# Attention and MLP on one core: sums in four column tiles, weights rounded in pieces of 768 columns

## The chip, the cores and the metric

The kernel runs on one core of a Trainium2 chip. The metric is the device time of one launch in microseconds. Five engines work beside each other: PE (matrix products), DVE and POOL (elementwise work[...]), ACT (activations, copies) and SP (issues the DMAs).

## What is computed

```python
# q, k, v: (8, 12, 448, 64); w_in: (768, 2048), w_out: (2048, 768); weights arrive as float64
q_n, k_n = rmsnorm(q, g_q), rmsnorm(k, g_k)
scores = q_n @ k_n.T / 8
attn = exp(scores - max) ; attn = attn / (sum(attn) + 1e-9)
x = (attn @ v), heads side by side          # (8 * 448, 768)
h = x @ w_in
out = (h - tanh(h)) @ w_out                 # (3584, 768)
```

## The kernel before

All values are held transposed: rows on the free axis, d (or the feature) on the partitions. There are 48 steps `s`, one for each pair of heads of each of the 8 batches, six pairs to a batch. A step's attention is cut into `norm` (squares on POOL, their sums on DVE, the power -1/2 on POOL), `norm_q` (q times its factor, DVE), `turn` (k and q transposed by PE, copied by ACT), `scores` (two halves, exponentials on ACT), `add` (sums of the exponentials over four chunks of keys, from step 8 on), `totals` (sums over keys by products with ones), `values` (products with v) and `divide`. The output of `divide` is `xT[b, hp]`, 128 rows (two heads of 64) by 448 queries; for the second three pairs of a batch it also forms the differences `tt` that the fast matrix product needs (on DVE for batch 0, on POOL later).

The MLP is a stream (`mlp`) of single matmuls: `hidden` and `project`, each made of sets of seven products of half size (Strassen-Winograd), 128x128 by 224 columns. A product's result is taken from PSUM by ACT or DVE (`use`). Batch 0's projection (`project_first`) uses plain matmuls of 448 columns instead, 96 of them, counted by `m`.

Everything is in an order written out by hand; each engine runs its own instructions in that order. Slots -3 to 5 (`first_slot`) hold batch 0's attention and no MLP. In slots 6 to 11 (`slot`) the attention of batch 1 is interleaved with batch 0's MLP, in slots 12 to 47 (`late_slot`) that of the following batches with the MLP of the batch before; `run(gap)` takes so much of the stream. The last batch's MLP follows alone.

The weights come as float64 words. A piece is loaded (`weight_load`), then rounded to float32 in three steps: `round_weight_a` on ACT (L71, L72), `round_weight_b` on DVE (L78, L79, L82), `round_weight_c` on POOL (L90). A piece has 384 columns of values; there are 64 of them, 32 of w_in and 32 of w_out. `weight(n)` does step a of piece n-1 and step b of the piece before it; `finish_weights` does step c, for the first `EARLY` = 16 pieces one piece further behind. These 16 are loaded into the place of the tile `gT`, the others into four buffers `w_raw`. In the small slots the number `ahead` says how far to go, later each product of batch 0 asks for its share (`due`). After eight pieces `combine_weights` forms the seven factors of a set; `keep_weights` writes them to DRAM.

The second half of `project_first` forms the factors of w_out: `combine_w_out` (L279, L281, L282 on DVE, L280 on POOL) at every fourth matmul, into slots of a ring of six tiles. Three of the seven factors are blocks of w_out itself; `keep_w_out` writes each of them to DRAM (192 KB) four pieces after it was rounded. The other four are written (`keep_factors`) one combination later. From batch 1 on the products read their factors from DRAM through the ring (`ring_load`), five tiles ahead; the first four loads are issued at m = 86.

In `first_slot` and `slot`, `totals` gives 128 rows by 448: each head's sums repeated over its 64 rows, so that one reciprocal (L427) and one product (L464) finish the step. In `late_slot`, `totals_by_halves` uses four column tiles of 32 and halves of the queries: 128 rows by 224, half the PE time and half the reciprocal (L442). Its rows do not stand where `divide` needs them, so `rows_out` writes four rows to DRAM and `rows_in` reads them back spread over 128 partitions.

Of the kernel before, what the change touches and what calls it, by code (L numbers as in the profile page):

```python
# [20 lines left out]
NCH = 4  # L21
# [71 lines left out]
def bounded_path(tc, ctx, q, k, v, moe_w_in, moe_w_out, out, g_col, ident, ones, neg_half):  # L93
# [14 lines left out]

    nc = tc.nc
# [11 lines left out]
    EARLY = 16  # L121
# [60 lines left out]
    NSTAGE = CF * S // DM  # L182
# [10 lines left out]
    def weight_piece(n):  # L193

        if n < 2 * CF:
            j, f, blk = n // 8, n % 8 // 4, n % 4
            p, low, i = ((1, 0, 0), (0, 1, 0), (4, 1, 1), (2, 0, 1))[blk]
            return 2 * j + f + low * HF, i, built(j, p)[:, f]
        i, f = 1 - (n - 2 * CF) // CF, n % CF
        if i == 0:  # L200
            f = f // 2 + f % 2 * HF
        return f, i, w_out_row(f, i)

    def weight_load(n):

        f, i, _ = weight_piece(n)
        if n < EARLY:
            raw = stage[:, n % NSTAGE * DM : (n % NSTAGE + 1) * DM].rearrange("p (f w) -> p f w", w=2)
        else:
            raw = wp.tile([P, HALF, 2], I32, name="w_raw", bufs=4)  # L210
        if n < 2 * CF:
            rows = w_in_words[i * HALF : (i + 1) * HALF, f * 2 * P : (f + 1) * 2 * P]
            nc.sync.dma_start(
                out=raw.rearrange("p (c f) w -> p c (f w)", c=HC),
                in_=rows.rearrange("(c p) f -> p c f", p=P),
            )
        else:
            nc.sync.dma_start(
                out=raw.rearrange("p f w -> p (f w)"),
                in_=w_out_words[f * P : (f + 1) * P, 2 * i * HALF : 2 * (i + 1) * HALF],  # L220
            )
        raws[n] = raw
# [4 lines left out]
    def place_free(n):  # L227

        if n < EARLY:
            return n - NSTAGE < done[2]  # L230
        return n - 4 < max(done[2], EARLY)

    def weight(to):

        while done[1] < min(to, 4 * CF):
            n = done[1]
            round_weight_a(nc, raws[n], weight_piece(n)[2])
            if n:
                round_weight_b(nc, raws[n - 1], weight_piece(n - 1)[2])
            done[1] = n + 1  # L240
            finish_weights(n - 1 if n < EARLY else n)
            while done[0] < min(n + 6, 4 * CF) and place_free(done[0]):
                weight_load(done[0])
                done[0] += 1
            if kept[1] < kept[0] and n >= 8 * kept[0] + 3:
                keep_weights()
        if done[1] == 4 * CF > done[2]:
            round_weight_b(nc, raws[4 * CF - 1], weight_piece(4 * CF - 1)[2])
            finish_weights(4 * CF)

    def finish_weights(to):
        while done[2] < to:
            round_weight_c(nc, raws.pop(done[2]), weight_piece(done[2])[2])
            done[2] += 1
            if done[2] % 8 == 0 and done[2] <= 2 * CF:
                combine_weights(done[2] // 8 - 1)
            keep_w_out(done[2] - 4)
# [15 lines left out]
    def combine_w_out(f):  # L273

        a11, a21 = (w_out_row(f, i) for i in range(2))
        a12, a22 = (w_out_row(f + HF, i) for i in range(2))
        t = [ring_slot() for _ in range(2)]
        s3, s1, s2, s4 = (t[i // 2][:, i % 2 * HALF : (i % 2 + 1) * HALF] for i in range(4))
        nc.vector.tensor_tensor(out=s1, in0=a21, in1=a22, op=ALU.add)  # L279
        nc.gpsimd.tensor_tensor(out=s3, in0=a11, in1=a21, op=ALU.subtract)  # L280
        nc.vector.tensor_tensor(out=s2, in0=s1, in1=a11, op=ALU.subtract)  # L281
        nc.vector.tensor_tensor(out=s4, in0=a12, in1=s2, op=ALU.subtract)  # L282
        late["keep"].append(lambda: [keep_factors(3 + 2 * i, 2, f, t[i]) for i in range(2)])

    def keep_factors(n, count, f, src):
        nc.sync.dma_start(
            out=w_out_dram[:, n : n + count, :, f, :].rearrange("p k c d -> p (k c) d"),
            in_=src[:, : count * HALF].rearrange("p (k d) -> p k d", d=P),
        )

    def keep_w_out(n):

        if not 2 * CF <= n < 4 * CF:
            return
        f, i, src = weight_piece(n)
        blk = {(0, 0): 0, (HF, 0): 1, (HF, 1): 2}.get((f // HF * HF, i))
        if blk is not None:
            keep_factors(blk, 1, f % HF, src)
# [106 lines left out]
    def values(s, av):  # L405
        v_nat = loaded.pop(("v", s))
        for c in range(NCH):
            p = probs[s, c // 2]
            for h in range(2):
                nc.tensor.matmul(  # L410
                    av[h * D : (h + 1) * D, :S], lhsT=v_nat[:, h, c, :], rhs=p[:, h, c % 2, :],
                    start=(c == 0), stop=(c == NCH - 1),
                )
        return av

    def totals(s, dn):
# [3 lines left out]
        for i, p in enumerate(parts):  # L420
            for h in range(2):
                nc.tensor.matmul(  # L422
                    dn[h * D : (h + 1) * D, :S], lhsT=ones[:CP, :D], rhs=p[:, h, :],
                    start=(i == 0), stop=(i == len(parts) - 1),
                )
        rd = whole[s] = sp.tile([P, S], F32, name="rd")
        nc.vector.reciprocal(rd, dn[:, :S])  # L427

    def totals_by_halves(s, dn):

        t = sums.pop(s)
        parts = t if t else [probs[s, c // 2][:, :, c % 2, :] for c in range(NCH)]
        for i, p in enumerate(parts):
            for h in range(2):
                for n in range(2):
                    r = (2 * h + n) * BL
# [7 lines left out]
    def rows_out(s):  # L444
        rs = whole[s]
        row = whole[s] = scratch.tile([2, S], F32, name="row", bufs=2)
        nc.sync.dma_start(
            out=row.rearrange("h (n q) -> (h n) q", n=2), in_=rs.rearrange("(g i) q -> g i q", i=BL)[:, 0, :]
        )

    def rows_in(s):

        row = whole[s]
        rd = whole[s] = sp.tile([P, S], F32, name="rd")
        nc.sync.dma_start(
            out=rd,
            in_=bass.AP(tensor=row.tensor, offset=row.offset, ap=[[S, 2], [0, D], [1, S]]),
        )

    def divide(s, av):  # L460
        b, hp = steps[s]
        rd = whole.pop(s)
        x = xT[b, hp] = xp.tile([P, S], F32, name="xT")
        nc.vector.tensor_tensor(  # L464
            out=x.rearrange("r (p c) -> r c p", c=NCH), in0=av[:, :S].rearrange("r (c p) -> r c p", c=NCH),
            in1=rd.rearrange("r (c p) -> r c p", c=NCH), op=ALU.mult,
        )
# [17 lines left out]

    due = [min(EARLY + m + 1, 3 * 8) for m in range(9)]
    due += [3 * 8 + m + 1 for m in range(8)]
    due += [2 * CF + CF * (m + 1) // 11 for m in range(11)]
    assert len(due) == 7 * SETS and due[-1] == 3 * CF
# [7 lines left out]
    def products(b, layer, count, width, depth, moving, done_with):  # L497
# [8 lines left out]
        def product(j, p, bank, first):  # L506
            if b == 0:
                weight(due[7 * j + ORDER.index(p)])
                w = built(j, p).rearrange("p f (c d) -> p (f c) d", d=P)
# [3 lines left out]
            for f in range(width):  # L513
                for c in range(depth):
                    nc.tensor.matmul(  # L515
                        bank[:, f * HS : (f + 1) * HS], lhsT=w[:, f * depth + c, :], rhs=moving[p](c),
# [19 lines left out]
    def hidden(b):  # L536
# [17 lines left out]
        def done_with(j):  # L554
            up, down = slice(2 * j, 2 * j + 2), slice(HF + 2 * j, HF + 2 * j + 2)
            s1, s2, s5, u3 = part("s1"), part("s2"), part("s5"), part("u3")
# [14 lines left out]
            def use(p, bank):  # L571
# [9 lines left out]
                elif p == 7:  # L581
                    nc.vector.tensor_tensor(out=u3, in0=v, in1=s5, op=ALU.add)
                    nc.vector.tensor_tensor(out=s1, in0=v, in1=s1, op=ALU.add)

                    def rest():
                        shrink(down, high, u3, nc.gpsimd)
# [31 lines left out]
    def project(b):  # L618
# [7 lines left out]
        def done_with(j):  # L626
            y1, y2, s1, s5 = (part(n).rearrange("p f s -> p (f s)") for n in ("s2", "u3", "s1", "s5"))

            def use(p, bank):
# [3 lines left out]
                elif p == 5:  # L633
                    nc.vector.tensor_tensor(out=s5[:, low], in0=v, in1=s1[:, low], op=ALU.add)
# [4 lines left out]
                elif p == 7:  # L639
                    nc.vector.tensor_tensor(out=y2[:, high], in0=v, in1=s5[:, low], op=ALU.add)  # L640
# [12 lines left out]
    def project_first(b):  # L653
# [6 lines left out]
        for m in range(CD * CF):  # L660
# [4 lines left out]
            if k < HC:  # L665
                weight(3 * CF + CF * (m + 1) // (HC * CF))
            elif m < HC * CF + 4:
                keep_w_out(4 * CF - 4 + m - HC * CF)
            elif (m - HC * CF) % 4 == 0 and m - HC * CF <= 4 * HF:
                for fn in late["keep"]:  # L670
                    fn()
                late["keep"] = []
                combine_w_out((m - HC * CF) // 4 - 1)
            elif m == CD * CF - 12:
                for fn in late["keep"]:
                    fn()
            elif m == CD * CF - 10:
# [13 lines left out]
    def mlp():  # L691
        late["todo"], late["keep"] = [], []
# [30 lines left out]
    def first_slot(s):  # L723
# [8 lines left out]
        ahead = 3 * (s + 4) if s < 0 else 9 + (EARLY - 9) * (s + 1) // NP  # L732
        weight(ahead - 2)
# [4 lines left out]
        weight(ahead - 1)  # L738
# [33 lines left out]
    def late_slot(s):  # L772
        gap = gap_ns(s)
        totals_by_halves(s, sc_bank())
# [5 lines left out]
        rows_out(s)  # L780
# [3 lines left out]
        rows_in(s)  # L784
# [15 lines left out]
    for n in range(4):  # L800
        weight_load(n)
    done[0] = 4
# [235 lines left out]
def kernel(  # L1038
# [45 lines left out]
    ones = consts.tile([P, D], F32, name="ones")  # L1084
# [41 lines left out]
```

## Time and profile before

| | |
|---|---|
| time, median of 3 | 1537.23 us (1536.94 to 1537.45) |
| the profiled execution | 1537.23 us, span 1535.0 us |
| busy PE | 1470.6 us |
| busy DVE | 783.0 us |
| busy POOL | 618.8 us |
| busy ACT | 425.7 us |
| DMA | 255.41 MB, mean 166 GB/s |

A matmul in float32 is recorded twice[...], so 16 records are 8 matmuls. In a timeline row the first number is the start in us from the span's start, the second the length of the merged group, then engine, line, operation, output<-inputs, shapes and how many; in brackets the idle time of the engine before it and what ended it. In a row of groups the numbers after the bar are busy us and mean ns of one, then the idle time before them. L numbers are lines of the kernel before.

### The profile page before, as it was taken

The page shows a single profiled execution, that of the slowest core. Times are in us where ns is not written, and L with a number is a line of the kernel's source. Part 1 is how long each engine was busy: PE and PEld are TensorE (multiplying, and loading weights), DVE is VectorE, ACT ScalarE, POOL GpSimd, SP SyncE. Part 2 cuts the span into 40 slices and gives each one's busy share as a digit, 9 for nine tenths or more (in the row PEclk, how much of TensorE's full clock was granted, in tenths as well). Part 3 has the DMA queues.
Part 4 walks back from the last instruction along what each step waited for, and adds up shares of the span by engine and source line. Part 5 has one row for each costly group of instructions (what it writes and reads, how often), then busy time and mean ns, then how long its engine had stood idle before and what let it go on. Part 6 is the DMA issues. An engine that isn't in the chain of part 4 may idle for free.

```text
span 1535.0 us, 20449 instructions
## 1 busy us (share of the span) xinstructions
PE 1470.6 (96%) x7584; PEld 1156.3 (75%) x7584; DVE 783.0 (51%) x1110; ACT 425.7 (28%) x817; POOL 618.8 (40%) x463
## 2 busy tenths in 40 slices
PE   3999879999999999999999999999999999999998
PEld 1346654448788788878878878887887887889997
DVE  6777888774544365345543455434543354432321
ACT  4463334422322133122221223212232132210100
POOL 5655556634443244432443333432453335311310
PEclk9999989999999999999999999999999999999999
DMA  7534557786456655565455564565556555456563
GB/s 193 160 99 158 179 173 188 190 240 188 159 161 167 172 160 162 154 184 166 147 177 159 165 180 149 159 165 172 161 159 179 151 165 165 138 154 179 181 199 100
DMA packets 255448, 255.41 MB, mean 166 GB/s; under 512 B 143324, under 2 KB 203756, under 8 KB 255340
## 3 DMA queue, kind: packets, MB, share of 16 engines
q1 hardware_dynamic: 255016, 254.01, 56.6%
q8 instruction: 63, 1.03, 0.3%
q14 instruction: 45, 0.37, 0.1%
q10 hardware_dynamic: 324, 0.00, 0.0%
HBM read 220.60 MB, written 33.36 MB: 165 GB/s over the span
## 4 chain that ended last, share of the span: by engine, by line
PE 75%; DVE 14%; DMA 4%; POOL 3%; issue 2%; SPq 2%; ACT 0%; DVEq 0%; ACTq 0%; POOLq 0%
PE mm L515 54%; PE sc L384 8%; PE sc L410 7%; DVE w_out L79 2%; POOL sq L337 1%; DVE rd L427 1%; DVE rr L338 1%; PE sc L437 1%; PE mm L422 1%; POOL rr L342 1%; DVE w_out L82 1%; PE mm L410 1%; DVE w_out L78 1%; PE sc L364 1%; DVE sum L403 1%
## 5 line engine op out<-in xcount | busy, mean ns | idle before, releaser
L389 ACT ACTIVATE p<-sc,rr 112x448 f32<-112x448 f32 x384 | 212.3, 636 | 483.4 <-PE sc L384 407.9
L515 PE MATMUL mm<-xT,w_f 128*128 128x224 f32 x1392 | 280.5, 356 | 4.7 <-DVE s L576 2.7
L515 PEld LDWEIGHTS mm<-xT,w_f 128*128 128x128 f32 x1392 | 261.3, 191 | 23.0 <-issue 14.6
L515 PEld LDWEIGHTS mm<-gT,w_f 128*128 128x128 f32 x1344 | 251.3, 190 | 23.7 <-issue 14.0
L515 PE MATMUL mm<-gT,w_f 128*128 128x224 f32 x1344 | 267.8, 355 | 0.0
L515 PE MATMUL mm<-tt,w_f 128*128 128x224 f32 x1044 | 215.6, 357 | 5.6 <-DVE gT L552 3.2
L515 PEld LDWEIGHTS mm<-tt,w_f 128*128 128x128 f32 x1044 | 197.1, 192 | 16.6 <-issue 8.0
L515 PE MATMUL mm<-tg,w_f 128*128 128x224 f32 x1008 | 200.4, 353 | 0.0
L515 PEld LDWEIGHTS mm<-tg,w_f 128*128 128x128 f32 x1008 | 189.5, 190 | 0.0
L384 PE MATMUL sc<-qT,kT 64*112 64x448 f32 x768 | 178.8, 574 | 9.1 <-DVE rd L427 6.4
L552 POOL TENSOR_TENSOR gT<-s,th 128x448 f32<-128x448 f32 x64 | 77.7, 1214 | 232.1 <-ACT th L551 232.1
L342 POOL TENSOR_TENSOR rr<-rr,neg_half 112x16 f32<-112x16 f32 (+1 forms) x49 | 140.0, 2857 | 51.0 <-DVE rr L341 50.0
L337 POOL TENSOR_TENSOR sq<-q_nat 112x512 f32<-112x512 f32 x48 | 50.0, 1041 | 255.5 <-DVE rr L338 247.3
L384 PEld LDWEIGHTS sc<-qT,kT 64*112 64x112 f32 x768 | 64.0, 176 | 103.8 <-issue 81.9
L410 PE MATMUL sc<-p,v_nat 112*64 112x448 f32 x672 | 135.2, 544 | 0.0
L464 DVE TENSOR_TENSOR xT<-sc,rd 128x448 f32<-128x448 f32 x42 | 40.7, 970 | 127.3 <-PE sc L410 115.1
L338 DVE TENSOR_REDUCE rr<-sq 112x8 f32<-112x512 f32 x96 | 64.9, 676 | 78.3 <-POOL sq L337 78.2
L403 DVE TENSOR_TENSOR sum<-sum,p 112x896 f32<-112x896 f32 x80 | 97.0, 1213 | 12.8 <-ACT p L389 7.9
L478 POOL TENSOR_TENSOR tt<-xT,tt 128x224 f32<-128x224 f32 x21 | 24.7, 1176 | 186.8 <-DVE xT L464 186.8
L410 PEld LDWEIGHTS sc<-p,v_nat 112*64 112x64 f32 x672 | 45.1, 137 | 71.7 <-issue 69.6
L679 PE MATMUL mm<-gT,w_out 128*128 128x448 f32 x192 | 76.1, 549 | 2.1 <-POOL w_out L90 2.1
L551 ACT ACTIVATE th<-s 128x448 f32<-128x448 f32 x64 | 37.1, 579 | 117.8 <-DVE s L595 57.7
(106 smaller groups left out, 1486.9 us busy)
## 6 DMA issues: line engine op xcount, KB each, us to landing
w_f<-w_in SPq DMA_DIRECT2D x196, 384.0 KB
w_f<-w_out SPq DMA_DIRECT2D x147, 512.0 KB
w_raw<-in_moe_w_out_dram SPq DMA_DIRECT2D x32, 384.0 KB
k_nat<-in_k_dram SPq DMA_DIRECT2D x96, 112.0 KB
q_nat<-in_q_dram SPq DMA_DIRECT2D x48, 224.0 KB
v_nat<-in_v_dram SPq DMA_DIRECT2D x48, 224.0 KB
out_dram<-th SPq DMA_DIRECT2D x192, 56.0 KB
w_in<-w_out SPq DMA_DIRECT2D x21, 384.0 KB
```

The lines of the kernel that those rows point to most:

```text
L337: nc.gpsimd.tensor_tensor(out=sq, in0=rows, in1=rows, op=ALU.mult)
L338: nc.vector.reduce_sum(rr[:, "kq".index(name)], sq, axis=AX.X)
L342: nc.gpsimd.tensor_tensor(out=r, in0=r, in1=neg_half[:, : r.shape[1]], op=ALU.pow)
L384: nc.tensor.matmul(sc[:CP, :S], lhsT=kT[r, c * CP : (c + 1) * CP], rhs=qT[r, :], start=True, stop=True)
L389: nc.scalar.activation(p[:, h, i, :], tiles[h][:CP, :S], AF.Exp, scale=rr[:, 0, 2 * c + h : 2 * c + h + 1])
L403: nc.vector.tensor_tensor(out=t, in0=t, in1=part, op=ALU.add)
L410: nc.tensor.matmul(av[h * D : (h + 1) * D, :S], lhsT=v_nat[:, h, c, :], rhs=p[:, h, c % 2, :], start=(c == 0), stop=(c == NCH - 1),)
L464: nc.vector.tensor_tensor(out=x.rearrange("r (p c) -> r c p", c=NCH), in0=av[:, :S].rearrange("r (c p) -> r c p", c=NCH), in1=rd.rearrange ...
L515: nc.tensor.matmul(bank[:, f * HS : (f + 1) * HS], lhsT=w[:, f * depth + c, :], rhs=moving[p](c), start=(first and f == 0 and c == 0), sto ...
L551: nc.scalar.activation(th, h, AF.Tanh, bias=0.0, scale=1.0)
L552: eng.tensor_tensor(out=g[:, rows, cols], in0=h, in1=th, op=ALU.subtract)
L679: nc.tensor.matmul(bank[:, :S], lhsT=w_out_row(f, n // HC)[:, n % HC * P : (n % HC + 1) * P], rhs=g[:, f, :], start=(f == 0), stop=(f == C ...
```

## The change

Four things are changed together.

- `values` uses four column tiles of 32 (two halves of d by two heads) instead of two of 64. Row (m, h, r) of x is then d = 32 m + r of head h; w_in's rows are loaded in that order, in four DMAs of 32 partitions per piece. `totals` of all slots uses four tiles by halves of the queries, rows (n, h). `divide` multiplies in four pieces of 64 rows by 224 queries, where the two inputs can be on different partitions. `rows_out` and `rows_in` are gone.
- A piece of weights has 768 columns: 32 pieces. `EARLY` is 8, `w_raw` has three buffers of twice the size. `finish_weights(n)` no longer lags in the early slots. `ahead` and `due` are set anew.
- `keep_w_out` is gone: `combine_w_out` writes all seven factors of a row, its own blocks among them, in five DMAs right behind it; it stands at every fifth matmul from m = 48. The first ring loads stand at m = 92.
- The tile `u3` is gone, `s5` is used in place.

```diff
-    EARLY = 16
+    EARLY, PIECES = 8, 2 * CF
-    NSTAGE = CF * S // DM
+    NSTAGE = CF * S // (2 * DM)
...
-            raw = wp.tile([P, HALF, 2], I32, name="w_raw", bufs=4)
+            raw = wp.tile([P, 2 * DM], I32, name="w_raw", bufs=3)
...
+            rows = w_in_words[i * HALF : (i + 1) * HALF, f * 2 * P : (f + 2) * 2 * P]
+            rows = rows.rearrange("(c h m r) f -> m h r c f", c=HC, h=2, m=2)
+            for r in range(4):
+                nc.sync.dma_start(
+                    out=raw[r * BL : (r + 1) * BL].rearrange("p (c f) -> p c f", c=HC), in_=rows[r // 2, r % 2]
+                )
...
-            finish_weights(n - 1 if n < EARLY else n)
-            while done[0] < min(n + 6, 4 * CF) and place_free(done[0]):
+            finish_weights(n)
+            while done[0] < min(n + 4, PIECES) and place_free(done[0]):
...
-            keep_w_out(done[2] - 4)
...
-        late["keep"].append(lambda: [keep_factors(3 + 2 * i, 2, f, t[i]) for i in range(2)])
+        for n, count, src in ((0, 1, a11), (1, 1, a12), (2, 1, a22), (3, 2, t[0]), (5, 2, t[1])):
+            nc.sync.dma_start(
+                out=w_out_dram[:, n : n + count, :, f, :].rearrange("p k c d -> p (k c) d"),
+                in_=src[:, : count * HALF].rearrange("p (k d) -> p k d", d=P),
+            )
...
-            for h in range(2):
-                nc.tensor.matmul(
-                    av[h * D : (h + 1) * D, :S], lhsT=v_nat[:, h, c, :], rhs=p[:, h, c % 2, :],
-                    start=(c == 0), stop=(c == NCH - 1),
-                )
+            for m in range(2):
+                for h in range(2):
+                    r = (2 * m + h) * BL
+                    nc.tensor.matmul(
+                        av[r : r + BL, :S], lhsT=v_nat[:, h, c, m * BL : (m + 1) * BL], rhs=p[:, h, c % 2, :],
+                        start=(c == 0), stop=(c == NCH - 1),
+                    )
...
-        nc.vector.tensor_tensor(
-            out=x.rearrange("r (p c) -> r c p", c=NCH), in0=av[:, :S].rearrange("r (c p) -> r c p", c=NCH),
-            in1=rd.rearrange("r (c p) -> r c p", c=NCH), op=ALU.mult,
-        )
+        for n in range(2):
+            for m in range(2):
+                nc.vector.tensor_tensor(
+                    out=x[m * D : (m + 1) * D].rearrange("r (p c) -> r c p", c=NCH)[:, 2 * n : 2 * n + 2],
+                    in0=av[m * D : (m + 1) * D, n * HS : (n + 1) * HS].rearrange("r (c p) -> r c p", c=2),
+                    in1=rs[n * D : (n + 1) * D].rearrange("r (c p) -> r c p", c=2), op=ALU.mult,
+                )
...
-    due = [min(EARLY + m + 1, 3 * 8) for m in range(9)]
-    due += [3 * 8 + m + 1 for m in range(8)]
-    due += [2 * CF + CF * (m + 1) // 11 for m in range(11)]
+    due = [EARLY + m // 2 + 1 for m in range(8)] + [12]
+    due += [12 + m // 2 + 1 for m in range(8)]
+    due += [CF + HF * (m + 1) // 11 for m in range(11)]
...
-            elif (m - HC * CF) % 4 == 0 and m - HC * CF <= 4 * HF:
-                for fn in late["keep"]:
-                    fn()
-                late["keep"] = []
-                combine_w_out((m - HC * CF) // 4 - 1)
...
-            elif m == CD * CF - 10:
+            elif (m - HC * CF) % 5 == 0 and m - HC * CF < 5 * HF:
+                combine_w_out((m - HC * CF) // 5)
+            elif m == CD * CF - 4:
                 ring_load(4)
...
-        ahead = 3 * (s + 4) if s < 0 else 9 + (EARLY - 9) * (s + 1) // NP
-        weight(ahead - 2)
+        ahead = (1, 3, 4, 4, 5, 6, 6, 7, 8)[s + 3]
+        weight(ahead - 1)
...
-        totals_by_halves(s, sc_bank())
+        totals(s, sc_bank())
...
-        rows_out(s)
...
-        rows_in(s)
```

## The prediction

> **What bounds the kernel now.** I read the page first, its slices, then busy time by stretch. The stretches are cut at the divisions (L464) that end a slot: 51.8 us is slot 0's, 107.4 slot 5's, 291.3 slot 10's; at 340.2 the late slots begin.
>
> ```profile
> PE   3999879999999999999999999999999999999998
> ...
> DVE  6777888774544365345543455434543354432321
> ```
>
> ```profile
> 0.00:51.80 51.80, 24.12 (x90) 10.72 (x92) 32.04 (x49) 20.30 (x40) 33.77 (x29) 0.93 0.63 172
> 51.80:107.40 55.60, 53.62 (x282) 20.82 (x284) 43.47 (x60) 31.59 (x63) 29.90 (x20) 1.00 0.48 148
> 107.40:291.30 183.90, 162.64 (x667) 106.02 (x667) 154.67 (x221) 81.00 (x164) 102.27 (x82) 0.94 0.60 177
> 291.30:340.20 48.90, 46.81 (x151) 22.11 (x150) 43.17 (x53) 11.14 (x22) 27.54 (x24) 1.00 0.68 188
> 340.20:1535.00 1194.80, 1183.45 (x6401) 996.58 (x6400) 509.67 (x730) 281.66 (x531) 425.37 (x311) 1.00 0.56 164
> ```
>
> Columns: stretch, length, busy time of PE, PEld, DVE, ACT, POOL, then clock, DMA share, GB/s. After 340 us PE is 99% busy: only PE work itself, or a new stall, counts there. Before it PE idles 46 us, and from 107 to 291 DVE is 84% busy. The timeline of DVE and POOL in slot 4 shows what one small slot hangs on:
>
> ```profile
> 97.93 0.68 DVE L348 TENSOR_TENSOR n<-q_nat,rr 112x512 f32<-112x512 f32 x1
> 98.53 0.35 DVE L78 TENSOR_SCALAR w_out<-w_out 128x384 f32<-128x384 f32 x1
> 98.92 0.36 DVE L79 TENSOR_SCALAR w_out<-w_out 128x384 int32<-128x384 int32 x1
> 99.31 0.56 DVE L82 SCALAR_TENSOR_TENSOR w_out<-gT,w_out 128x384 int32<-128x384 int32 x1
> 99.79 0.68 DVE L338 TENSOR_REDUCE rr<-sq 112x8 f32<-112x512 f32 x1
> 101.62 0.69 DVE L338 TENSOR_REDUCE rr<-sq 112x8 f32<-112x512 f32 x1 [1.15 <-POOL sq L337]
> ...
> 105.75 1.05 DVE L79 TENSOR_SCALAR w_out<-w_out 128x384 int32<-128x384 int32 x1
> ```
>
> ```profile
> 94.86 1.04 POOL L337 TENSOR_TENSOR sq<-k_nat 112x512 f32<-112x512 f32 x1
> ...
> 105.53 1.05 POOL L90 TENSOR_TENSOR w_out<-w_out,gT 128x384 int32<-128x384 int32 x1
> ```
>
> The square of k (94.86) is done long before its sum (99.79), since no rounding stands ahead of it on POOL. And L79 takes 0.36 alone, 1.05 beside L90. In the middle slots the order is another; the chain of waits there:
>
> ```profile
> 157.52 0.70 DVE w_out L78
> 158.22 1.33 issue
> ...
> 160.52 1.05 POOL sq L337
> ...
> 161.60 0.70 DVE rr L338
> 162.36 1.05 POOL sq L337
> ```
>
> The rounding's last addition (L90), then both squares, stand in series with DVE. Durations, by shape:
>
> ```profile
> L427 DVE RECIPROCAL rd<-mm 128x448 f32<-128x448 f32 x6 | 17.7, 2955 | 1.8 <-PE mm L422 1.8
> ...
> L442 DVE RECIPROCAL rs<-sc 128x224 f32<-128x224 f32 x36 | 56.0, 1555 | 10.9 <-PE sc L437 10.9
> ...
> L464 DVE TENSOR_TENSOR xT<-sc,rd 128x448 f32<-128x448 f32 x42 | 40.7, 970 | 127.3 <-PE sc L410 115.1 <-DMA rd<-row 11.6
> ...
> L641 DVE TENSOR_TENSOR s<-mm,s 128x224 f32<-128x224 f32 x21 | 8.0, 381 | 0.0
> ```
>
> And two rows of PE's timeline, four tiles of 32 and two of 64:
>
> ```profile
> 725.85 0.59 PE L437 MATMUL sc<-sum,ones 112*32 112x224 f32 x8
> 710.21 3.23 PE L410 MATMUL sc<-p,v_nat 112*64 112x448 f32 x16
> ```
>
> [...]
>
> **Part by part.** The sum is in the span, 1535.0 us; the profiled execution took 1537.23 with 2.2 us around it, which is also the median.
>
> *Sums over values (48 slots).* 32 records in quads in place of 16 in pairs. A pair starts every 0.375 us (3.16 to the next group), L437's quads start as fast: 0. If not, see the last rival. *Sums over keys.* Slots 0 to 7: 3.16 becomes 8 quads of 224, 1.6, saving 1.58 each; slots 8 to 11: 0.81 to 0.52. PE loses 13.8 us, which counts only where PE sets the slot. Late slots: same matmuls, 0.
>
> *Reciprocal and division.* Twelve reciprocals fall by 1.4. Each division becomes four of 64x224 to a strided output. 0.970 against 0.622 unstrided at 448 puts stride at 0.35, so 0.175 at 224: 0.39 + 0.175 = 0.56, and 0.49 from start to start: 2.04 in place of 0.87, +1.2 on DVE (bounds: 1.5 to 2.4 in all).
>
> *DMA.* 36 rows out and 36 in go, with SP's waits for the reciprocal. The idle column of PE's groups names no DMA there: 0. w_in's loads become 64 issues for 32, at about 0.45 us 13 us more on SP over 230 us; v and k loads stand behind them, but a slot or more ahead of use, which hides it: 0 (all 13 if that lead were gone). The 24 own-block writes of w_out (19 of them before 291) move behind the first half of the projection.
>
> *Double pieces (768 columns).* Alone a piece costs DVE 1.22 us from start to start[...]. POOL's addition has no visible fixed part: 1.05 becomes 2.1. And `finish_weights(n)` puts piece n-1's addition right behind its DVE steps in the early slots too, where it lagged a piece. It blocks POOL's next squares.
>
> Stage by stage:
>
> 1. *To slot 0's division (51.8).* Before, two and three single pieces stand ahead of the first two norms' products (L348: 16.4, 26.9, 38.5 us). Now it is none, one double, none. The second then starts near 24: its sums are scaled by 20.6 (22.2 before, POOL's squares starting 1.2 earlier), the double rounding beside POOL's power takes some 3.2. Two double additions hold POOL to 29.7, so the third norm's sums are scaled at 33.3 (33.8 before) and its product, with no piece between, comes at 36.5 instead of 38.5 and unhindered by additions (L348 took 2.45 there): PE goes on at 37.3, not 41.1. The sums over keys take 2.4 there for 4.8, but the reciprocal waits for DVE's sums to 45.3, and the division comes at about 47.3: -4.5 (bounds -7, +1).
> 2. *Slots 0 to 5 (55.6).* A slot with a double: division 2.04, L348 0.6, rounding 2.1, addition 2.2, squares and sums 3.8, reciprocal 1.5 = 12.3; from slot 3 on tt adds 1.3: 13.7. Without a double PE sets it: 10.0, or 11.2 with tt. Doubles end slots 1, 2, 4; slot 1 also has the combination with its POOL step, +2.4. So 10.0 + 14.7 + 12.3 + 11.2 + 13.7 = 61.9: +6.3 (bounds 0, +10).
> 3. *Slot 5 to 6 (22.8).* Three doubles, where four single pieces were left: 2 more single pieces' work, 2.4, and the longer addition ahead of the norm, 1.0; less 0.2: +3.2.
> 4. *Slots 6 to 10 (161.1).* 42 pieces become 21: -8.4. [...] The addition ahead of the squares, +1.0 in four slots; two combinations beside a longer addition, +1.0. Reciprocal and division together -0.2 in four. DVE's two waits behind late weights (3.7 and 2.5) shrink, -1.5: with three doubles in place of four pieces in flight loads lead little more. Sum -5.7 (bounds -18, +4).
> 5. *To 340.* DMA share 0.68 of 48.9 is 33 us. 19 writes more, 384 packets of 512 bytes at 27 ns over 16 engines, 0.65 us each: +12.3, together 0.93. The combinations (every five matmuls, not four) need ring slots back from such writes; the first ring tile stands behind them. Its load stands at m = 92, not 86, behind k and q: +2.5 (bounds -1, +9).
> 6. *Late slots.* Behind the division wait the sums (L401, L403) and products' results. Two products, 4.5 us, cover them; the queue grows from 4.4 to 5.6 us. Half of the 36 slots divide in the hidden layer with its short products, and one in seven of them by 1 us: +2.5 (bounds -2, +15).
>
> Sum: -4.5 + 6.3 + 3.2 - 5.7 + 2.5 + 2.5 = +4.3. Span 1539.3, time 1541.5: slower by 0.3%. Measurement can't tell 0.2% (3.1 us) from no change.
>
> **Rivals.**
> *DVE's relief wins.* If norms rarely follow a fresh piece, POOL's addition is off the chain: stages 2 and 3 cost 0 and -1, stage 4 about -10.5, the rest -4.5 + 1 + 0: -15, time 1522. For it: DVE is the bound there. Against: the chain above shows L90 ahead of the squares. It decides once stages 2 to 4 together cost 7.3 us less than in my sum.
> *Late stalls.* If each late division costs PE 0.5 us: 18 in place of 2.5, time 1557. Against: the L515 groups waited 16 us in the whole run (4.7, 5.6, 5.9), most of it before 340.
> *Write burst.* If the writes back up 10 us ahead of the ring's first tile: 1549. For: DMA share 0.93. Against: the first ring load was issued at 336.8 and its product began at 342.5, 5.7 us of cover.
> *The tiles don't do it.* If quads ran as two pairs at 448: 48 x 3.0 = +144, 1681. L437 speaks against.
>
> **How the numbers follow.** Likeliest (1541.5, own range 1534 to 1549) 0.45; relief 0.28; late stalls 0.13; burst 0.11; tiles and others 0.03. Range 1521 to 1557: from relief to late stalls. Faster: 0.25 of relief and 0.03 of the likeliest, 0.28. Same: 0.13 of the likeliest and 0.03 of relief, 0.16. Slower: 0.56.
>
> **What would show it.** The first division at about 47 us; the sixth at 109; DVE waiting over 3 us for POOL's squares in slots 2 and 5; the seventh division near 135; late slots at PE 99% with 3.2 us for 32 records. Wrong: POOL's squares still early in the small slots, or L79 waiting less per column than now.

## The result and the profile after

| | before | changed |
|---|---|---|
| time, median of 4 runs | 1537.3 us (1536.94 to 1537.45) | 1551.87 us (1551.0 to 1554.08) |
| ratio, 95% interval | | 1.0097 (1.008 to 1.0115) |
| the profiled execution, span | 1535.0 us | 1552.1 us |

The changed kernel is 14.6 us slower. The profiled execution of it was the slowest of the four (1554.08 us), so the stages below add up to 17.1 us in the span. The two or three us too many can lie in the first stretches, which vary between kernels that are the same there (50.1, 48.3 and 49.0 us to the first division in three of them).

Cut at the same events as in the prediction (the divisions are L434 now, four records each; L numbers in a view are lines of the kernel that it shows), in us:

| stage | before | after | difference | forecast |
|---|---|---|---|---|
| 1. to slot 0's division | 51.8 | 50.1 | -1.7 | -4.5 |
| 2. to slot 5's | 55.6 | 67.9 | +12.3 | +6.3 |
| 3. to slot 6's | 22.8 | 25.9 | +3.1 | +3.2 |
| 4. to slot 10's | 161.1 | 147.4 | -13.7 | -5.7 |
| 5. to the first late slot's sums | 48.9 | 55.1 | +6.2 | +2.5 |
| from there to the first product of batch 1 | 2.3 | 13.6 | +11.3 | in 5 |
| 6. the rest | 1192.5 | 1192.1 | -0.4 | +2.5 |

Two views of the profile after show it: the slices, and the busy time by stretch (columns as before: PE, PEld, DVE, ACT, POOL, then clock, DMA share, GB/s).

```profile
PE   3778889997999999999999999999999999999998
...
DVE  3658888873545456435654455544653555532321
```

```profile
50.10:118.00 67.90, 53.35 (x451) 22.67 (x451) 44.47 (x66) 33.74 (x60) 33.73 (x20) 0.90 0.58 148
118.00:143.90 25.90, 18.89 (x126) 13.34 (x124) 21.13 (x26) 9.76 (x16) 13.60 (x8) 0.89 0.13 31
143.90:291.30 147.40, 132.69 (x647) 89.01 (x648) 123.22 (x141) 63.37 (x97) 86.83 (x51) 0.93 0.62 183
291.30:346.40 55.10, 51.75 (x181) 24.57 (x179) 47.50 (x56) 11.96 (x21) 32.10 (x23) 0.94 0.70 190
346.40:360.00 13.60, 2.33 (x17) 0.80 (x17) 2.89 (x3) 2.74 (x5) 1.44 (x2) 0.74 0.99 258
360.00:1552.00 1192.00, 1181.89 (x6960) 992.84 (x6960) 565.78 (x835) 278.52 (x526) 442.77 (x310) 1.00 0.54 157
```

PE has 14.6 us without work in the small slots (0 to 5), where it had 2.0, and its clock is 0.90 there in place of 1.00. From 346.4 to 360.0 PE does 2.33 us of work while the DMA engines are full. The late slots are as long as before, though their divisions take DVE 1.4 us more each.

**The wait of 11.3 us.** SP's timeline ahead of the late slots, and PE's at their start:

```profile
287.57 0.70 SPq L220 DMA_DIRECT2D w_raw<-in_moe_w_out_dram  x1
304.64 1.90 SPq L584 DMA_DIRECT2D out_dram<-th  x4
306.59 1.57 SPq L290 DMA_DIRECT2D w_out<-w_out  x3
...
345.48 3.84 SPq L584 DMA_DIRECT2D out_dram<-th  x4
349.36 1.58 SPq L290 DMA_DIRECT2D w_out<-w_out  x3
351.05 1.11 SPq L290 DMA_DIRECT2D w_out<-w_f  x2
352.25 2.46 SPq L163 DMA_DIRECT2D k_nat<-in_k_dram  x2
354.76 0.68 SPq L166 DMA_DIRECT2D q_nat<-in_q_dram  x1
355.48 1.88 SPq L318 DMA_DIRECT2D w_f<-w_in  x4
```

```profile
346.97 1.76 PE L379 MATMUL sc<-qT,kT 64*112 64x448 f32 x8
360.02 2.21 PE L486 MATMUL mm<-xT,w_f 128*128 128x224 f32 x5 [11.29 <-DMA w_f<-w_in]
```

SP stood 16.3 us at an output's store (L584 at 304.64, which waits for DVE's transposition th), and no write of w_out could be issued in that time. All 24 own blocks came behind it. The ring's first load was issued at 355.48, and its product followed 4.5 us later. In the kernel before, the same load and its product:

```profile
336.84 3.33 SPq L323 DMA_DIRECT2D w_f<-w_in  x4
...
342.46 2.54 PE L515 MATMUL mm<-xT,w_f 128*128 128x224 f32 x12
```

The busy time by stretch says what SP's wait left idle and what came after it, first in the changed kernel, then in the kernel before:

```profile
287.60:304.60 17.00, 13.65 (x38) 6.32 (x37) 15.43 (x18) 5.97 (x9) 12.03 (x9) 0.92 0.24 67
304.60:320.00 15.40, 15.40 (x45) 7.82 (x45) 14.92 (x19) 3.90 (x7) 9.56 (x6) 0.87 0.71 190
320.00:346.40 26.40, 26.40 (x110) 12.28 (x108) 19.60 (x25) 3.79 (x7) 13.18 (x11) 1.00 1.01 275
```

```profile
287.60:301.00 13.40, 11.31 (x34) 5.02 (x33) 12.99 (x17) 5.51 (x11) 9.27 (x9) 1.00 0.47 156
301.00:320.00 19.00, 19.00 (x68) 8.69 (x67) 17.29 (x23) 3.80 (x7) 11.19 (x8) 1.00 0.86 231
320.00:340.20 20.20, 20.20 (x63) 9.85 (x62) 16.45 (x18) 3.80 (x7) 9.97 (x8) 1.00 0.73 205
```

In the changed kernel the DMA share is 0.24 in the 17 us in which SP waited, then 0.71, then 1.01: the DMA engines first had little to do and then were full until 360. Before, the share was 0.73 when the ring's loads were issued. The store waited because th stands behind the last roundings on DVE, which was busy for 15.43 of those 17.0 us. That this wait made the burst is read from the trace; what an experiment below tests is the place of the writes.

**The small slots.** DVE and PE in slots 3 and 4, from their timelines:

```profile
89.25 2.32 DVE L434 TENSOR_TENSOR xT<-mm,rs 64x224 f32<-64x224 f32 x4
91.61 0.60 DVE L448 TENSOR_TENSOR tt<-xT 128x224 f32<-128x224 f32 x1
...
93.16 0.69 DVE L343 TENSOR_TENSOR n<-q_nat,rr 112x512 f32<-112x512 f32 x1
...
98.19 1.56 DVE L426 RECIPROCAL rs<-mm 128x224 f32<-128x224 f32 x1 [1.70 <-PE mm L421]
104.19 1.17 DVE L434 TENSOR_TENSOR xT<-mm,rs 64x224 f32<-64x224 f32 x2 [4.45 <-PE mm L407]
```

```profile
93.99 0.98 PE L359 MATMUL sc<-ident,n 112*128 112x112 f32 x4 [3.16 <-DVE n L343]
94.90 3.22 PE L421 MATMUL mm<-p,ones 112*32 112x224 f32 x32
98.05 2.93 PE L379 MATMUL sc<-qT,kT 64*112 64x448 f32 x8
...
109.20 1.72 PE L421 MATMUL mm<-p,ones 112*32 112x224 f32 x32
```

In the kernel before, in slot 4:

```profile
98.76 0.57 PE L364 MATMUL sc<-ident,n 112*128 112x112 f32 x4 [0.84 <-DVE n L348]
99.26 3.23 PE L422 MATMUL mm<-p,ones 112*64 112x448 f32 x16
```

No piece is rounded in slot 3, and still it took 14.9 us in this execution (14.8 and 13.4 in the profiles of two runs below, whose code is the same there). Division (2.3) and tt stand ahead of n (L343), and PE waits 3.16 us for n where it had waited 0.84. Then the sums over keys take 3.22 us, as long as in the old form, where the same 32 records take 1.72 one slot later. PE's clock is 0.77 in this slot and 1.00 in the next. That the wait brought the lower clock is a guess from their order; it is not tested, and after a wait of 2.35 us in the next slot the clock did not fall. The reciprocal, shorter by 1.4, ends at 99.8; the division waits till 104.19 for the values. Its gain is beside PE.

**The relief in stage 4.** Groups of one engine by shape, the rounding of w_out, and L79 in the kernel before:

```profile
L90 POOL TENSOR_TENSOR w_out<-w_out,w_raw 128x768 int32<-128x768 int32 x20 | 41.9, 2095 | 46.2 <-DVE w_out L82 21.2 <-issue 9.5 <-ACT w_out L71 5.7
...
L79 DVE TENSOR_SCALAR w_out<-w_out 128x768 int32<-128x768 int32 x28 | 27.1, 969 | 1.0
L82 DVE SCALAR_TENSOR_TENSOR w_out<-w_raw,w_out 128x768 int32<-128x768 int32 x20 | 21.5, 1075 | 0.7
L78 DVE TENSOR_SCALAR w_out<-w_out 128x768 f32<-128x768 f32 x28 | 21.3, 759 | 0.1
```

```profile
L79 DVE TENSOR_SCALAR w_out<-w_out 128x384 int32<-128x384 int32 x56 | 43.3, 773 | 1.9
```

A double piece took DVE 0.76 + 0.97 + 1.08 = 2.8 us. All rows of L78, L79 and L82 together: 118.3 us before for 64 pieces (1.85 each), 87.0 now for 32 (2.72 each). Two effects are in this. Alone, a double piece takes 2.06 us from start to start where two single ones take 2 x 1.22, 0.38 less. And less time went beside POOL: in stage 4, L79 took longer than alone (0.36 us, 0.56 for a double piece) in 21 of 42 pieces before and in 7 of 20 double ones after, each time while an instruction ran on POOL, and what it took above that fell from 15.2 to 7.4 us.

### The profile page after: what moved, and what is told of

Its sections match the earlier page's. It is cut to its first block, busy times and chain, and to the rows that moved or that the text cites. A ratio compares the mean times of both kernels' runs of the same rounds, so it can differ in the third digit from the quotient of the medians.

```text
span 1552.1 us, 22055 instructions
## 1 busy us (share of the span) xinstructions
PE 1463.1 (94%) x8496; PEld 1153.6 (74%) x8496; DVE 823.5 (53%) x1158; ACT 419.0 (27%) x753; POOL 636.5 (41%) x431
## 4 chain that ended last, share of the span: by engine, by line
PE 75%; DVE 10%; POOL 4%; issue 4%; DMA 2%; SPq 1%; ACT 1%; DVEq 0%; POOLq 0%; ACTq 0%
PE mm L486 56%; PE sc L379 8%; PE sc L407 7%; POOL sq L332 2%; DVE rr L333 1%; POOL rr L337 1%; PE sc L421 1%; DVE xT L434 1%; DVE w_out L79 1%; DVE rs L426 1%; PE sc L359 1%; DVE sum L398 1%; POOL gT L523 1%; PE sc L355 1%; DVE w_out L82 1%
## 5 line engine op out<-in xcount | busy, mean ns | idle before, releaser
L486 PE MATMUL mm<-xT,w_f 128*128 128x224 f32 x1392 | 282.2, 357 | 16.5 <-DMA w_f<-w_in 11.3
L523 POOL TENSOR_TENSOR gT<-s,th 128x448 f32<-128x448 f32 x96 | 120.7, 1264 | 262.9 <-ACT th L522 262.9
L486 PEld LDWEIGHTS mm<-tt,w_f 128*128 128x128 f32 x1044 | 195.5, 190 | 12.5 <-issue 8.0
L434 DVE TENSOR_TENSOR xT<-sc,rs 64x224 f32<-64x224 f32 x168 | 94.0, 559 | 128.0 <-PE sc L407 123.7
L407 PE MATMUL sc<-p,v_nat 112*32 112x448 f32 x1344 | 134.8, 542 | 0.0
L449 POOL TENSOR_TENSOR tt<-xT,tt 128x224 f32<-128x224 f32 x21 | 29.0, 1381 | 208.3 <-DVE xT L434 208.3
L398 DVE TENSOR_TENSOR sum<-sum,p 112x896 f32<-112x896 f32 x80 | 107.3, 1342 | 9.1 <-ACT p L384 0.8
L522 ACT ACTIVATE th<-s 128x448 f32<-128x448 f32 x96 | 55.5, 579 | 169.9 <-DVE s L562 62.7
L407 PEld LDWEIGHTS sc<-p,v_nat 112*32 112x32 f32 x1344 | 40.0, 109 | 72.7 <-issue 70.0
```

The costliest lines, as they stand in the source:

```text
L398: nc.vector.tensor_tensor(out=t, in0=t, in1=part, op=ALU.add)
L407: nc.tensor.matmul(av[r : r + BL, :S], lhsT=v_nat[:, h, c, m * BL : (m + 1) * BL], rhs=p[:, h, c % 2, :], start=(c == 0), stop=(c == NCH - 1),
L434: nc.vector.tensor_tensor(out=x[m * D : (m + 1) * D].rearrange("r (p c) -> r c p", c=NCH)[:, 2 * n : 2 * n + 2], in0=av[m * D : (m + 1) * ...
L486: nc.tensor.matmul(bank[:, f * HS : (f + 1) * HS], lhsT=w[:, c * width + f, :], rhs=moving[p](c), start=(first and f == 0 and c == 0), sto ...
L522: nc.scalar.activation(th, h, AF.Tanh, bias=0.0, scale=1.0)
L523: eng.tensor_tensor(out=g[:, rows, cols], in0=h, in1=th, op=ALU.subtract)
```

## The experiments

All times are medians, each beside runs of the kernel before on the same chip (1537.06 to 1537.65 us). "The five slots" is the time from slot 0's division to slot 5's: 55.6 us before, 67.9 in the changed kernel.

**The addition behind its rounding again a piece late.**

```diff
-            finish_weights(n)
+            finish_weights(n - 1 if n < EARLY else n)
```

> The changed kernel, but the last step of the rounding (POOL's addition) of the first eight pieces lags one piece again, so that it no longer stands between a fresh DVE rounding and the squares. Theory A (the addition ahead of k's square is what lengthens the small slots, and PE's lower clock there, 0.74 to 0.77 in two slots, follows from PE's waits): from the first to the sixth division 67.9 us becomes 57 to 61, those slots run at clock 0.95 or more, and the whole falls by 6 to 11 us, to about 1543. Rival B (DVE's own work is what is longer: four divisions of 0.59 us and a double piece in one slot): 67.9 stays above 65 and the whole above 1549.

1548.22 us, five slots 61.9, their clock 0.92. Between the two: 6.0 us of the 12.3 go in the slots as profiled, 3.7 in the medians of the whole (the changed kernel was profiled in its slowest execution, this one in its fastest). The order of POOL's addition is part of the cause, at most half of it; slots 3 and 4 stay at 13.3 us each, and ahead of the first of them PE waits 3.5 us for n.

**Own blocks written as they are rounded.**

```diff
+            keep_w_out(done[2] - 2)
...
-        for n, count, src in ((0, 1, a11), (1, 1, a12), (2, 1, a22), (3, 2, t[0]), (5, 2, t[1])):
+        for i in range(2):
+            keep_factors(3 + 2 * i, 2, f, t[i])
```

> The changed kernel, but w_out's own blocks are written to DRAM two pieces after they are rounded, as before, and a combination writes only its four sums. Theory W (24 writes of 192 KB crowd the 50 us ahead of the first ring loads): PE's wait of 11.3 us for w_f falls under 3 us, the division before the late slots comes no later, and the whole falls by 8 to 13 us, to about 1541. Rival V (the DMA volume only moves, and the loads of w_raw in slots 7 to 10 wait for it instead): the 11.3 us go, but the stretch from the seventh to the eleventh division (147.4 us) grows by 6 us or more, and the whole stays above 1547.

1542.59 us, 9.3 less than the changed kernel. From the start of PE's last projection matmul to the first product of batch 1: 4.7 us (14.0 in the changed kernel, 2.7 before). PE's wait for w_f there is 1.99 us. Stage 4 took 147.7 us, as long as without the writes, though its DMA share rose from 0.62 to 0.69. Theory W holds: the place of the 24 writes costs 9.3 us, and in stage 4 there was room for them. What is left of the wait is the place of the loads, still behind k and q in SP's timeline:

```profile
339.87 1.00 SPq L294 DMA_DIRECT2D w_out<-w_f  x2
340.96 2.14 SPq L163 DMA_DIRECT2D k_nat<-in_k_dram  x2
343.15 0.67 SPq L166 DMA_DIRECT2D q_nat<-in_q_dram  x1
343.87 1.88 SPq L332 DMA_DIRECT2D w_f<-w_in  x4
```

**The first ring loads at m = 86.**

```diff
-            elif m == CD * CF - 4:
+            elif m == CD * CF - 10:
```

> The changed kernel, but the first four ring loads are issued at m = 86 again, ahead of the loads of k and q. Theory Q (the loads are late because they stand last in SP's queue; what stands just ahead of them, k and q and a part of the stores, is 3 to 4 us): PE's wait of 11.3 us falls by 3 to 4, the whole to about 1548. Rival D (the DMA engines are full, share 0.97 to 1.03 from 320 us on, so an earlier issue lands no earlier): the wait falls by less than 1 us and the whole stays within 1 us of the changed kernel.

1550.64 us, 1.2 less, which is within the spread of the runs (1549.17 to 1552.25 here, 1551.0 to 1554.08 there); the same stretch 13.0 for 14.0. SP's timeline has the loads ahead of k and q now, and they still come late:

```profile
347.64 1.57 SPq L290 DMA_DIRECT2D w_out<-w_out  x3
349.33 1.11 SPq L290 DMA_DIRECT2D w_out<-w_f  x2
350.49 3.45 SPq L318 DMA_DIRECT2D w_f<-w_in  x4
```

Rival D is the nearer one: behind the full DMA engines of this kernel an earlier place in the queue gained about 1 us. With the own blocks out of the way it closes the rest of the gap (below).

**x by halves alone.** The kernel before with the new values, totals, division and order of w_in's rows; pieces of 384 and all writes as before.

```diff
...
-        totals_by_halves(s, sc_bank())
+        totals(s, sc_bank())
...
-        rows_out(s)
...
-        rows_in(s)
```

> The kernel before with only x's rows by halves of d: four column tiles of 32 for values and totals in all slots, four divisions, no rows through DRAM, w_in loaded in four parts per piece; pieces of 384 columns and the writes of own blocks as before. By the stages measured (late slots 1192.1 against 1192.5 us): the late slots gain nothing; in the small slots DVE's reciprocal falls by 1.4 and the division grows by 1.4, PE's totals fall by 1.5, so that the five slots after the first division take 52 to 56 us (55.6 before) and the whole 1532 to 1538. Rival (four divisions and 64 loads on SP cost by themselves, and part of the 12.3 us is theirs): the five slots take 60 us or more and the whole 1542 or more.

1542.21 us, ratio 1.003 (1.0019 to 1.0042): 4.6 of the 14.6 us. The five slots take 60.6 us, 12.6 + 11.1 + 10.3 + 13.3 + 13.3; stage 4 took 163.3 (161.1 before), the rest 1190.3 (1192.5). The rival's figures came. This run prices the new order of rows as a whole: values, sums, reciprocal, four divisions and 64 loads; which of them lengthens the small slots, the run with one wide division tells. The relief of stage 4 in the changed kernel doesn't come from the order of rows, nor from the writes (147.7 with them early), so it comes with the double pieces and their schedule.

**n ahead of the division.** Tried on three kernels and in a sum of edits.

```diff
+        if has(s + 3):
+            norm_q(s + 3)
         if has(s):
             divide(s, values(s, mm_bank()))
-        if has(s + 3):
-            norm_q(s + 3)
```

> The changed kernel, but in the slots -3 to 5 q's product with its factor (n) stands ahead of the division on DVE instead of behind it. Theory P (in the small slots the division, 2.3 us for 0.9, and the four tt stand between the values and n, PE waits for n, 11.1 us in three waits, and then runs for some us at a clock of 0.6; the reciprocal that became 1.4 us shorter lies beside PE's values and gains nothing): the five slots fall from 67.9 to 59 to 63 us, and the whole by 5 to 9, to about 1545. Rival A2 (n waits for the power of POOL, late because of the addition ahead of the squares, wherever n stands): under 2 us.

> The kernel before with x's rows by halves of d alone (1542.2 us, five small slots 60.6), and n ahead of the division in the slots -3 to 5. Theory P: the two waits of 2.4 us for n and the low clock behind them go, the five slots take 53 to 56 us, the whole 1535 to 1538. Rival (ACT's copies of k and q, with 3.4 us of waits beside, set the slots as well): 58 us or more and the whole above 1540.

> The kernel before with n ahead of the division in the slots -3 to 5, nothing else. Theory P: with a division of 0.9 us PE waited only 2.0 us for n in the five slots, so at most 2 us are to be had: 1535 to 1537.5. Rival: the place of n is worth as much here as in the changed kernel (5 us or more): 1532 or less.

The changed kernel with it: 1555.24 us (1554.11 to 1556.69), 3 to 4 more than without it, five slots 67.1. x by halves alone with it: 1541.29, five slots 60.5. The kernel before with it: 1534.47, ratio 0.9981 (0.9973 to 0.9989), five slots 54.0; that is 2.6 us, a little above the 2 that theory P allowed. Theory P falls as I had put it: where the division is long, its place gives nothing. DVE's timeline of x by halves alone, with n first, and POOL's, show why:

```profile
85.39 1.49 DVE L349 TENSOR_TENSOR n<-q_nat,rr 112x512 f32<-112x512 f32 x1 [1.49 <-POOL rr L343]
86.80 2.35 DVE L440 TENSOR_TENSOR xT<-mm,rs 64x224 f32<-64x224 f32 x4
...
91.77 0.68 DVE L339 TENSOR_REDUCE rr<-sq 112x8 f32<-112x512 f32 x1
93.60 0.69 DVE L339 TENSOR_REDUCE rr<-sq 112x8 f32<-112x512 f32 x1 [1.15 <-POOL sq L338]
...
97.58 1.49 DVE L349 TENSOR_TENSOR n<-q_nat,rr 112x512 f32<-112x512 f32 x1 [1.49 <-POOL rr L343]
```

```profile
94.64 2.90 POOL L343 TENSOR_TENSOR rr<-rr,neg_half 112x16 f32<-112x16 f32 x1 [1.07 <-DVE rr L342]
97.51 1.01 POOL L90 TENSOR_TENSOR w_out<-w_out,gT 128x384 int32<-128x384 int32 x1
```

From one n to the next is 12.2 us, and it is a closed ring on two engines: n, division, tt, rounding, sums with POOL's square of q between them, power, n. With n behind the division the ring is another (division, tt, n, turn, sums over keys, scores, values, division), but the division is in both. In this order n also runs beside POOL's addition (97.51) and takes 1.49 us for 0.69.

**All mended, four divisions kept.** The lag, own blocks early, loads at m = 86, n first.

> The changed kernel with four edits together: POOL's addition lags a piece in the first eight pieces, w_out's own blocks are written as they are rounded, the first ring loads stand at m = 86, n stands ahead of the division in the slots -3 to 5. If the causes add: 1551.9 - 3.7 (the lag, measured) - 9.3 (own blocks, measured) - 1 (ring) - 5 to 9 (n) = 1529 to 1533, faster than the kernel before by 4 to 8 us. If the small slots only have one gain to give, whichever edit takes it: 1535 to 1538.

1536.56 us, ratio 0.9998 (0.9989 to 1.0007): no different from the kernel before. The wait for the ring is gone (2.7 us, as before), the five slots take 63.7. With the lag alone they took 61.9, so n first added nothing there. The second forecast, one gain whichever edit takes it, was right for the small slots.

**One wide division in the small slots.** To test the ring: slots -3 to 5 form the sums over keys 448 wide in four column tiles with rows (m, h), so that one reciprocal of 448 and one division of 128x448 fit the new order of rows.

```diff
+        if s < NP:
+            for i, p in enumerate(parts):
+                for m in range(2):
+                    for h in range(2):
+                        r = (2 * m + h) * BL
+                        nc.tensor.matmul(
+                            dn[r : r + BL, :S], lhsT=ones[:CP, :BL], rhs=p[:, h, :],
+                            start=(i == 0), stop=(i == len(parts) - 1),
+                        )
+            rd = whole[s] = part("s5").rearrange("p f s -> p (f s)")
+            nc.vector.reciprocal(rd, dn[:, :S])
+            return
...
+        if s < NP:
+            nc.vector.tensor_tensor(
...
```

> The kernel before with x's rows by halves of d alone, but in the slots -3 to 5 the sums over keys are formed 448 wide (four column tiles, rows (m, h)), so that one reciprocal of 448 and one division of 128x448 serve the new order of rows; from slot 6 on halves and four divisions. Theory L (the division stands in a loop whichever side of n it has: values, division, n, turn, sums, scores, values, or n, division, rounding, sums, power, n; the four of them make the loop 1.4 us longer and drop PE's clock, the shorter reciprocal stands beside PE): the five slots go back from 60.6 to 55 to 57 us, the whole to 1536 to 1538.5. Rival (the 64 loads of w_in, or values in tiles of 32, lengthen the slots): they stay above 59 and the whole above 1541.

1538.78 us, ratio 1.001 (1.0001 to 1.0018), about 3 less than with four divisions; five slots 58.5, between the 55 to 57 of theory L and the 59 of the rival (the profiled execution, 1541.01 us, was one of the two slowest of 12). DVE's timeline:

```profile
98.81 0.99 DVE L451 TENSOR_TENSOR xT<-mm,s 128x448 f32<-128x448 f32 x1 [1.88 <-PE mm L413]
...
100.96 0.69 DVE L349 TENSOR_TENSOR n<-q_nat,rr 112x512 f32<-112x512 f32 x1
```

Slots 3 and 4 are 11.6 us again, exactly as before, for 13.3 with four divisions, though DVE's reciprocal takes 2.96 us for 1.56 and PE's sums over keys are twice as wide: PE's waits for n fall from 4.8 us to 1.7, and n follows the start of the division by 2.15 us (3.69 with four). The loads and the values in tiles of 32 are as in the run with four divisions, and sums and reciprocal got longer, so only the division can be the gain. Theory L holds for the slots that wait for n. Slot 0 is still long (14.1 for 11.3): there PE waited 1.8 us for ACT's copy kT, and the 32 records of the sums took 4.91 us, where the values' 32 of the same width took 3.21. Why that wait comes with the new order was not tried.

> The changed kernel with the lag, own blocks written as rounded, the ring loads at m = 86, and the wide sums with one division in the slots -3 to 5 (n behind the division). Theory L: five slots 56 to 58 us (61.9 with the lag alone), the whole 1531 to 1535, below the kernel before. Rival (the double pieces hold the slots by themselves): 61 or more, the whole 1537 or more.

> As the run before, with n ahead of the division in the slots -3 to 5, which gave the kernel before 2.6 us. If it adds: 1529 to 1533, faster than the kernel before by 4 us or more. If the double piece now stands in the loop n, division, rounding, sums, power: no gain, or a loss of 1 to 3 us, against the run before.

Both with the other three edits. Without n first: 1533.78 us, ratio 0.9978 (0.9971 to 0.9985), as theory L said for the whole, but five slots 61.7, as the rival said. With n first: 1530.84 us, ratio 0.9957 (0.9942 to 0.9971), five slots 60.3. The last is faster than both kernels, by 6.3 us against the one before. It keeps the double pieces (stage 4: 148.2 us), has no wait for the ring (2.8 us), and its small slots are still 4.7 us longer than before. The 56 to 58 us expected of them did not come. x by halves alone gave 58.5 with the same wide division, so some 3 us are of that order of rows and the others of the double pieces; they were not taken apart further. Whether n first adds is near the limit of these runs: the two intervals just touch.

## Why the prediction was right, and where it was not

The direction was right and the time lay in the range. The sum of the likeliest case, +4.3 us, was too small by 10, and its own range (1534 to 1549) did not hold the time: what came is near the rival called write burst, to which 0.11 had been given. The working was right in part by luck. Stages 1 to 4 were forecast at -0.7 us in all and came at 0.0 only because two misses cancelled, +6.0 in stage 2 and -8.0 in stage 4; the net of the span, 17.1 us, is what stage 5 lost with the wait at its end, 17.5. Without the burst, in the run with the own blocks early, the kernel took 1542.59 us, near the 1541.5 of the likeliest case and still slower than before.

1. *To slot 0's division, -4.5:* it was -1.7, within the bounds. The step took POOL to be free of the second double addition at 29.7; that addition began at 30.92, the third norm's squares followed it, and n came at 39.5 in place of 36.5.
2. *Slots 0 to 5, +6.3:* it was +12.3, outside the bounds. Slot by slot 10.4, 16.3, 12.5, 14.9, 13.8 against the forecast 10.0, 14.7, 12.3, 11.2, 13.7: the slots with doubles were close, and POOL's addition ahead of the squares is what the lag's run showed it to be. The largest miss is slot 3, "without a double PE sets it". The working let PE keep its pace there, but with tt the longer division stands ahead of n: PE waits 3.16 us, and its clock is 0.77 in that slot. The term of PE's totals (1.6 us for 3.16) was right where the clock was 1.00 (1.72, slot 4) and gained nothing.
3. *Slot 5 to 6, +3.2:* +3.1, as stated.
4. *Slots 6 to 10, -5.7:* -13.7, within the bounds. The wrong term is the rounding: -8.4 us for 42 pieces. It took 0.4 us off for each of 21 double pieces, which was my estimate, and left the time lost beside POOL as it was. DVE's time from the start of each rounding instruction to the next, summed over the stretch, was 74.5 us for 42 pieces before and 55.2 for 20 double ones after, 19.3 less. One double more than I had counted had moved out of the stretch (about 2.8); the rest is more than a double saves alone (0.38, near the estimate), so the time lost beside POOL fell too, and "L79 waiting less per column than now", a sign that had been named as showing the forecast wrong, came (15.2 us above its time alone over 42 x 384 columns, 0.94 ns a column; then 7.4 over 20 x 768, 0.48). Alone a piece costs 1.22: 0.55 above it for each of the 42, 0.7 above 2.06 for each of the 20. Against that, waits for POOL's squares rose from 13.8 to 17.1 us, near the 4 foreseen.
5. *To 340, +2.5:* +17.5 with the wait at its end. This is the step that failed. It named the mechanism, with the ring's first tile behind such writes, and sized it at 2.5. The DMA time of a write, 0.65 us, is borne out: with the writes early, stage 4's share rose by 0.07 of 147.7 us, about 10 us for the 16 or so of them that lie in it. Share 0.93 was right as a mean over 49 us; but a mean hides that SP stood 16.3 us at a store first, so that the same writes met the ring's loads. "5.7 us of cover" was gone. The run with the writes early gave 9.3 us back. Of the 6.2 us ahead of the wait 2.8 are also in x by halves alone (51.7 for 48.9); the others were not taken apart.
6. *Late slots, +2.5:* -0.4; PE was without work for 10.1 of the 1192 us. The divisions are covered by products also where they are short; the rival of late stalls had no part in it.

Of the rivals, the relief came in stage 4 (13.7 where it gave 10.5) and not in the small slots; the burst came in full (11.3 for 10); the column tiles run four abreast (3.2 us for 32 records of the values, as for 16 in pairs before). Of the signs, DVE's waits for POOL's squares came in slots 2 and 5 (4.2 and 4.1 us, for 1.2 and 3.3 before), and the late slots kept PE at 99%; the first, sixth and seventh divisions came at 50.1, 118.0 and 143.9 for 47, 109 and 135. One reading of the profile before was off: its columns give 53 us in which PE has no work before 340, not 46. So a loss of 12 us, a gain of 14 and a burst of 11 lay behind a forecast of 4.

## What to carry to other kernels

A gain on DVE or PE counts only in the loop that sets the slot: here a reciprocal got shorter beside PE's values, and a division got longer between the values and the next turn. Write that loop down instruction by instruction, in both orders of its members, before a cost is set against a gain. When transfers are moved, look at what stands ahead of them in the issuing queue and sum the DMA time from the moment they can start to the moment the first load behind them is needed, not over the stage.

## What was not expected of the hardware

- PE's slow stretches followed waits that were rather short. The PE timelines of four runs show it (the changed kernel, the lag, x by halves alone without and with n first). Where PE had waited for 0.98 to 1.29 us ahead of q's turn in the small slots, the next 32 records of sums over keys in four column tiles took 1.72 us in eight of nine cases (2.25 in the other). After waits of 1.64 to 7.02 us they took 2.5 to 3.2 us in eight of nine, and 1.72 in one (after 2.35 us). By my count in the profiles of the other runs 1.72 also followed waits of 1.78, 2.37 and 2.55 us. Why these were not slow, no run shows.
- POOL's addition over 768 columns took 1.83 us alone where 384 took 1.01, so by an estimate from these two it has a fixed part of about 0.2 us (2 x 1.01 - 1.83); the prediction took 2.1.
- A division of 64x224 from PSUM to a strided output started every 0.59 us (0.49 was estimated), also the two of the four whose inputs stand on different partitions (2.34 us for the four of slot 0).
